# Strided sparse attention and a multiplicative FFN on one core: another order of work at the head

## The chip, the core and the metric

The kernel runs on one core of a Trainium2 chip. TensorE (PE in the profile; PEld is its weight load) multiplies and transposes into PSUM, VectorE (DVE) and ScalarE (ACT) read PSUM and write SBUF, GpSimd (POOL) here casts SBUF to SBUF and sets up masks, SyncE (SP) issues the loads; ACT issues the stores. The metric is device time in microseconds (us) of the one launch, lower is better. One execution is also taken with the profiler; its view gives every instruction a start and a length.

## The reference

Attention over 8 batches of 8 heads, 576 positions of 64 elements; the first four heads see a local band of 32 positions, the other four positions with the same remainder by 32. Its output, laid out as 4608 tokens of 512, goes through a feed-forward part without a nonlinearity but with a product of two projections:

```python
mask_local = (rel >= 0) & (rel < 32)
mask_strided = (rel >= 0) & (pos[None, :] % 32 == pos[:, None] % 32)
scores = np.where(masks[None], q @ k.T / sqrt(64), -1e9)
attn = softmax(scores)
x = (attn @ v).transpose(0, 2, 1, 3).reshape(4608, 512)
a = x @ w1            # 512 x 1024
b = x @ w2            # 512 x 1024
out = (a * b) @ w3 @ w_out    # 1024 x 1024, 1024 x 512
```

All inputs and the output are float32; the kernel computes its products in float16 with sums in float32.

## The kernel before

**Tiles.** Tokens go in nine tiles of 512, batches in eight of 576 tokens, and a batch in four *pairs* of heads: pairs 0 and 1 are local, 2 and 3 strided. w3 and w_out are multiplied once, in the kernel (the *fold*), so that each tile needs three sets of products: a and b (`ab_halves`, sixteen units of four matmuls), and the output products (`o_halves`, eight units of four).

**Loads.** Every load goes through one of nine staging buffers (`stgp`): a DMA issued by SP, then a cast to float16 on POOL or ACT. `load_w3(jc)` takes 128 rows of w3 (4 KB each) into one of four buffers `w3n`; `load_wo(g)` takes 512 KB of w_out in 2 KB rows; `load_w12(g)` takes 256 columns of w1 and of w2, 512 KB each in 1 KB rows, with w1's cast on ACT and w2's on POOL; `load_qk(b, grp)` takes q and k of four heads (512 KB each), `load_rest(b)` the last 64 positions of q and k of all heads, `load_vL` and `load_vS` take V for the local and the strided heads. `load_vL` also has a copy on DVE (line 187) that shifts rows of V after its casts on POOL (line 186).

**Fold.** `fold_tr(jc)` transposes a block of w3 on PE (line 465) and copies it out on DVE and ACT (lines 467, 468); `fold_mm(jc)` gives two half units of four matmuls each (line 443 in the shared helper `acc_halves`) and a copy of the result into `w34`.

**Attention of batches 0 and 1.** `ah_T` transposes q and k of a pair (line 320) and copies them into `qT` and `kT` on ACT; `ah_R` does the same for the rest of a batch. `ah_S` computes the scores in two groups (line 356), the exponential on ACT (line 360) and the mask product on DVE (line 361); `ah_PV` multiplies by V (line 374), and `norm` divides on DVE (lines 384, 385). `ph_T2` transposes the result (line 392) and copies it into `xT`, on ACT for these batches. Scores and products with V share two PSUM buffers (`psB`). The transposes of a pair and the back-transposes share a single one (`psM`), and fold, a, b and output products three (`psF`).

**Order.** PE runs in the order of the program text: each PE instruction is passed to `pe`. The attention of all batches is a list of steps, `stream`; `spread(units, upto, lead)` issues matmul units and, between them, steps of the stream evenly up to position `upto`, where the first `lead` units go without steps. The other engines' instructions are put in order by the framework. Loads go on SP in the order of the text.

In the kernel before, the loads start with w3's block 0 and w_out, then the other blocks of w3 are mixed with batch 0's q, k, v; then come w1 and w2, mixed with batch 1's. The fold is spread over batch 0's attention, then tile 0's a, b products and output products over batch 1's. Tile 1 begins after that, with batch 2's attention between its units, and so on.

In a batch of the stream, pair i's scores come before the back-transposes of pair i - 1, then its products with V, and the transposes of pair i + 2. From batch 2 on another set of functions is used (`ph_...`).

Of the kernel before, what the change touches and what calls it, by code (L numbers as in the profile page):

```python
# [8 lines left out]
FP32 = mybir.dt.float32  # L9
FP16 = mybir.dt.float16  # L10
# [9 lines left out]
def kernel(  # L20
# [11 lines left out]
    nc = tc.nc  # L32
    B, H, S, D = q.shape
# [3 lines left out]
    P = 128  # L37
    NT = 512
    NTILE = NTOK // NT
    KM = DM // P  # L40
    KF = DF // P
# [8 lines left out]
    NM = 512  # L50
# [21 lines left out]
    def copy(eng, out, in_):  # L72
        if eng == "a":
            nc.scalar.copy(out=out, in_=in_)  # L74
        elif eng == "v":
            nc.vector.tensor_copy(out=out, in_=in_)  # L76
        else:
            nc.gpsimd.tensor_copy(out=out, in_=in_)  # L78
# [65 lines left out]
    def load_w3(jc, eng):  # L144
        st = stgp.tile([P, DF], FP32, tag="stg")
        nc.sync.dma_start(st, moe_w3[bass.ds(jc * P, P), :])
        t = ffn.tile([P, DF], FP16, tag="w3n", bufs=4)
        w3n[jc] = t
        copy(eng, t, st)

    def load_w12(g):
        cs = bass.ds(g * 256, 256)
        for wd, wh, eng in ((moe_w1, w1h, "a"), (moe_w2, w2h, "p")):
            st = stgp.tile([P, KM, 256], FP32, tag="stg")
            nc.sync.dma_start(st, wd.rearrange("(c p) n -> p c n", p=P)[:, :, cs])
            copy(eng, wh[:, :, cs], st)


    x16 = {}
# [1 line left out]
    def load_qk(b, grp, engs="pp"):  # L161
        for nm, ten, eng in (("q", q, engs[0]), ("k", k, engs[1])):
            st = stgp.tile([P, 4, 4, D], FP32, tag="stg")
            nc.sync.dma_start(st.rearrange("p h c d -> p h (c d)"),
                              ten[b, 4 * grp:4 * grp + 4, 0:NM].rearrange("h (p c) d -> p h (c d)", c=4))
            t = qkp.tile([P, 4, 4, D], FP16, tag=f"{nm}{grp}")
            copy(eng, t, st.rearrange("p h c d -> p c h d"))
            x16[(b, nm, grp)] = t

    def load_rest(b, eng="p"):  # L170
        st = stgp.tile([P, H, D], FP32, tag="stg")
        for i, ten in enumerate((q, k)):
            nc.sync.dma_start(st[64 * i:64 * i + 64], ten[b, :, NM:S].rearrange("h p d -> p h d"))
        t = qkp.tile([P, H, D], FP16, tag="r")
        copy(eng, t, st)
        x16[(b, "r")] = t

    def load_vL(b):
        vt = v16L[b % 2]
        for hp in range(2):  # L180
            hs = slice(2 * hp, 2 * hp + 2)
            st = stgp.tile([P, 2, LT, D], FP32, tag="stg")
            for h in range(2):
                nc.sync.dma_start(st[32:P, h], v[b, 2 * hp + h].rearrange("(t p) d -> p t d", p=LQ))
            for pr in (bass.ds(32, 32), bass.ds(64, 64)):
                nc.gpsimd.tensor_copy(out=vt[pr, hs, :, 0:D], in_=st[pr])  # L186
            nc.vector.tensor_copy(out=vt[0:32, hs, 1:LT, 0:D], in_=vt[96:P, hs, 0:LT - 1, 0:D])

    def load_vS(b):
        vt = v16S[b % 2]  # L190
        for hp in range(2):
            st = stgp.tile([SQ, 2, ST, D], FP32, tag="stg")
            sf = st.rearrange("p h c d -> p h (c d)")
            sv = v[b, 4 + 2 * hp:6 + 2 * hp].rearrange("h (p c) d -> p h (c d)", c=ST)
            nc.sync.dma_start(sf[0:64], sv[0:64])
            nc.sync.dma_start(sf[64:SQ], sv[64:SQ])
            nc.gpsimd.tensor_copy(out=vt[:, 2 * hp:2 * hp + 2, :, 0:D], in_=st)  # L197
# [114 lines left out]
            norm(s, xps[0:w, :, 0:l * 65], cs[0], l)  # L312

    def ah_T(s):
        ps = psM.tile([P, 2, NM], FP16, tag="m")
        for i, nm in enumerate("qk"):
            src = x16[(s.b, nm, s.hp // 2)]
            h0 = 2 * (s.hp % 2)
            for c in range(4):
                pe(nc.tensor.transpose(ps[:, i, c * P:(c + 1) * P],  # L320
                                       src[:, c, h0:h0 + 2].rearrange("p h d -> p (h d)"), id16))
        for i, t in enumerate((qT, kT)):
            if s.local:
                c0 = 32 * i
                nc.scalar.copy(out=t[:, s.hp, c0:c0 + NM].rearrange("x (p c) -> x p c", c=4),
                               in_=ps[:, i].rearrange("x (c p) -> x p c", c=4))
            else:
                nc.scalar.copy(out=t[:, s.hp, 0:S].rearrange("x (u c w) -> x u c w", u=2, c=4)[:, :, :, 0:64],
                               in_=ps[:, i].rearrange("x (c t u) -> x u c t", c=4, u=2))

    def ah_R(b):
        ps = psM.tile([P, 4, 2, 128], FP16, tag="m")
        pv = ps.rearrange("x g a w -> x (g a w)")[:, 0:512].rearrange("x (g a w) -> x g a w", g=4, a=2)
        src = x16[(b, "r")]
        for g in range(4):
            pe(nc.tensor.transpose(pv[:, g].rearrange("x a w -> x (a w)"),
                                   src[:, 2 * g:2 * g + 2].rearrange("p h d -> p (h d)"), id16))
        for i, t in enumerate((qT, kT)):
            c0 = 32 * i + NM
            nc.scalar.copy(out=t[:, 0:2, c0:c0 + NR], in_=pv[:, 0:2, i])  # L340
            nc.scalar.copy(out=t[:, 2:4, 0:S].rearrange("x g (c w) -> x g c w", w=SQ)[:, :, :, 64:SQ],
                           in_=pv[:, 2:4, i].rearrange("x g (s c) -> x g c s", c=ST))

    def ah_ptm(s, g):
        return ptms[s.hp % 2][:, g * PTG:(g + 1) * PTG]
# [115 lines left out]
    def fold_tr(jc):  # L461
        js = bass.ds(jc * P, P)
        ps = psF.tile([P, 1024], FP16, tag="f", name="trp")
        for kc in range(KF):
            pe(nc.tensor.transpose(ps[:, kc * P:(kc + 1) * P], w3n[jc][:, bass.ds(kc * P, P)], id16))
        pv = ps.rearrange("x (c j) -> x c j", j=P)
        nc.vector.tensor_copy(out=w3T[0][:, :, js], in_=pv[:, 0:4, :])
        nc.scalar.copy(out=w3T[1][:, :, js], in_=pv[:, 4:8, :])
# [13 lines left out]
    def add(f, *a):  # L482
        stream.append(lambda: f(*a))
# [6 lines left out]
    def ph_TS(s, t):  # L490
# [8 lines left out]
        for f in after:  # L499
            f()  # L500

    for p, s in enumerate(pairs):
        b, i = divmod(p, 4)
        if b < AHEAD:
            if i == 0:
                add(ah_T, s)
                add(ah_R, b)
                add(ah_T, pairs[p + 1])
            add(ah_S, s)
            if i:  # L510
                add(ph_T2, pairs[p - 1])
            add(ah_PV, s, 0)
            add(ah_PV, s, 1)
            if i < 2:
                add(ah_T, pairs[p + 2])
            if i == 3:
                add(ph_T2, s)
                batch_end[b] = len(stream)
            continue
        if i == 0 and b == AHEAD:  # L520
            add(ph_TS, None, s)
            gaps(2)
        t = pairs[p + 1] if p + 1 < len(pairs) else None
        add(ph_TS, s, t)
        gaps(1)
        if i or b > AHEAD:
            add(ph_T2, pairs[p - 1])
            if i == 0:
                gaps(1)
                batch_end[b - 1] = len(stream)  # L530
        gaps(1 if i == 0 and b > AHEAD else 2)
        add(ph_PV, s)
        gaps(3)
        if p + 1 == len(pairs):
            add(ph_T2, s)
            batch_end[b] = len(stream)
    pos = [0]

    def spread(units, upto, lead=0):
        n = len(units) - lead  # L540
        p0 = pos[0]
        for i, u in enumerate(units):
            u()
            tgt = p0 + ((upto - p0) * max(i + 1 - lead, 0)) // n
            while pos[0] < tgt:
                stream[pos[0]]()
                pos[0] += 1
# [14 lines left out]
                    x()  # L562


    load_w3(0, "p")
    for g in range(4):
        load_wo(g, "p")
    load_w3(1, "p")
    load_qk(0, 0)
    load_rest(0)  # L570
    load_w3(2, "p")
    load_vL(0)
    load_w3(3, "p")
    load_qk(0, 1)
    load_w3(4, "p")
    load_w3(5, "p")
    load_vS(0)
    load_w3(6, "p")
    load_w3(7, "p")
    load_w12(0)  # L580
    load_w12(1)
    load_w12(2)
    load_qk(1, 0)
    load_rest(1)
    load_w12(3)
    load_vL(1)
    load_qk(1, 1)
    load_vS(1)

    fold = []  # L590
    fold_tr(0)
    for jc in range(KF):
        h0, h1 = fold_mm(jc)
        fold.append(h0)
        if jc + 1 < KF:
            fold.append(lambda jc=jc: fold_tr(jc + 1))
        fold.append(h1)
    spread(fold, batch_end[0], lead=3)
    load_qk(2, 0)
    load_rest(2)  # L600
    load_vL(2)
    units = ab_halves(0) + o_halves(0)
    p0, n = pos[0], batch_end[1] - 1 - pos[0]
    spread(units[0:16], p0 + n * 11 // 19, lead=4)
    load_qk(2, 1)
    load_vS(2)
    spread(units[16:23], p0 + n)
    units[23]()
    stream[pos[0]]()
    pos[0] += 1  # L610
    for tch in range(1, NTILE):
# [47 lines left out]
```

## Time and profile before

| | us |
|---|---|
| median of 3 timed runs | 296.75 (292.37, 296.75, 299.54) |
| the profiled execution | 292.48 |
| span of its instructions | 290.8 |
| start of tile 1's first product | 79.97 |

The busy shares of the span are 91% on PE, 52% each on DVE and ACT, 36% on POOL. The loads move 38.8 MB in, the stores 9.44 MB out. The chain that ended last is 73% PE, 10% ACT, 6% DMA and 6% DVE. The page of the profile shows the span in 40 equal slices of 7.3 us; a digit is the busy share in tenths. The timeline and the groups name an operation by engine, line, output and inputs, shapes (partitions x elements) and count; what stands in brackets is the idle time before and what ended it. A matmul's shown length includes its latency, so the pace of PE is read from the starts of successive ones. "PEclk" or granted clock is the share of TensorE's full clock that the records show.

### The profile page before, as it was taken

The page shows a single profiled execution, that of the slowest core. Times are in us where ns is not written, and L with a number is a line of the kernel's source. Part 1 is how long each engine was busy: PE and PEld are TensorE (multiplying, and loading weights), DVE is VectorE, ACT ScalarE, POOL GpSimd, SP SyncE. Part 2 cuts the span into 40 slices and gives each one's busy share as a digit, 9 for nine tenths or more (in the row PEclk, how much of TensorE's full clock was granted, in tenths as well). Part 3 has the DMA queues.
Part 4 walks back from the last instruction along what each step waited for, and adds up shares of the span by engine and source line. Part 5 has one row for each costly group of instructions (what it writes and reads, how often), then busy time and mean ns, then how long its engine had stood idle before and what let it go on. Part 6 is the DMA issues. An engine that isn't in the chain of part 4 may idle for free.

```text
span 290.8 us, 6556 instructions
## 1 busy us (share of the span) xinstructions
PE 264.0 (91%) x2617; PEld 136.8 (47%) x2617; DVE 150.0 (52%) x293; ACT 151.3 (52%) x305; POOL 103.4 (36%) x118
## 2 busy tenths in 40 slices
PE   2478998879899998999999999999999999999995
PEld 1134564445445554554555455545554554444442
DVE  2014764255747846576476577646645653330320
ACT  2025795827565465656555555565565555323332
POOL 6759544475466536675381535100000000000000
PEclk9997999979999999999999999999999999999999
DMA  7999999999699979996999670120021003003003
GB/s 242 357 224 340 293 348 249 230 267 209 195 291 233 211 172 286 243 243 173 265 265 216 186 216 1 63 87 0 2 80 68 2 0 140 7 0 147 1 0 144
DMA packets 58655, 48.66 MB, mean 167 GB/s; under 512 B 29184, under 2 KB 49664, under 8 KB 58624
## 3 DMA queue, kind: packets, MB, share of 16 engines
q1 hardware_dynamic: 53440, 38.81, 55.0%
q10 hardware_dynamic: 5184, 9.44, 8.9%
q8 instruction: 20, 0.33, 0.5%
q14 instruction: 11, 0.09, 0.1%
HBM read 38.80 MB, written 9.44 MB: 166 GB/s over the span
## 4 chain that ended last, share of the span: by engine, by line
PE 73%; ACT 10%; DMA 6%; DVE 6%; issue 3%; SPq 1%; POOL 0%; ACTq 0%
PE ops L443 22%; PE bps L429 20%; PE aps L420 19%; DMA st<-in_moe_w_dram 3%; PE sps L310 3%; DMA st<-in_moe_w_out_dram 3%; PE ps L392 2%; PE sps L268 2%; ACT xT L399 2%; ACT pte L360 2%; DVE xqs L385 1%; PE pt L225 1%; ACT pte L288 1%; ACT osb L454 1%; PE pt L268 1%
## 5 line engine op out<-in xcount | busy, mean ns | idle before, releaser
L420 PE MATMUL aps<-xT,w1h 128*128 128x512 f16 x288 | 76.2, 382 | 4.3 <-ACT xT L399 4.1
L423 ACT COPY asb<-aps 128x512 f32<-128x512 f32 x72 | 42.5, 590 | 63.8 <-PE aps L420 61.5
L429 PE MATMUL bps<-xT,w2h 128*128 128x512 f16 x288 | 74.3, 380 | 0.0
L431 DVE TENSOR_TENSOR abt<-bps,asb 128x512 f16<-128x512 f32 x72 | 49.5, 688 | 44.9 <-PE bps L429 42.9
L443 PE MATMUL ops<-w,abt 128*128 128x512 f16 x288 | 68.5, 379 | 0.0
L78 POOL CAST t<-st 128x1024 f16<-128x1024 f32 (+1 forms) x48 | 48.5, 1015 | 39.1 <-DMA st<-in_k_dram 21.6
L429 PEld LDWEIGHTS <-w2h 128*128 128x128 f16 x288 | 26.6, 98 | 35.3 <-issue 6.5
L443 PEld LDWEIGHTS <-abt 128*128 128x128 f16 x288 | 25.9, 98 | 27.1
L420 PEld LDWEIGHTS <-w1h 128*128 128x128 f16 x288 | 25.8, 98 | 25.4 <-issue 0.6
L454 ACT COPY osb<-ops 128x512 f32<-128x512 f32 x36 | 21.3, 592 | 29.9 <-PE ops L443 27.3
L186 POOL CAST v16L<-st 32x768 f16<-32x768 f32 (+1 forms) x32 | 27.5, 861 | 16.5 <-DMA st<-in_v_dram 8.5
L288 ACT ACTIVATE pte<-sps 128x960 f16<-128x960 f32 (+1 forms) x24 | 23.8, 990 | 11.8 <-PE sps L268 10.8
L385 DVE TENSOR_TENSOR xqs<-sps,rcp 96x768 f16<-96x768 f32 (+1 forms) x24 | 24.5, 1020 | 0.5
L197 POOL CAST v16S<-st 72x1024 f16<-72x1024 f32 x16 | 16.9, 1059 | 18.2 <-PE pm L310 13.8
L443 PE MATMUL ops<-woh,w3T 128*128 128x512 f16 x64 | 20.2, 446 | 1.7 <-POOL woh L78 1.1
L289 DVE TENSOR_TENSOR ptm<-pte,maskL 128x1152 f16<-128x1152 f16 x12 | 10.0, 832 | 21.8 <-ACT pte L288 21.8
L289 DVE TENSOR_TENSOR ptm<-pte,maskS 72x1152 f16<-72x1152 f16 x12 | 10.2, 854 | 19.5 <-ACT pte L288 19.5
L74 ACT COPY qT<-pt 128x256 f16<-128x256 f16 (+2 forms) x48 | 17.5, 409 | 0.9 <-DVE kT L76 0.9
L310 PEld LDWEIGHTS <-ptm 72*128 72x128 f16 (+1 forms) x336 | 13.6, 97 | 6.3 <-issue 0.6
L392 PEld LDWEIGHTS <-xqs 72*128 72x128 f16 (+1 forms) x224 | 11.9, 98 | 8.8 <-DVE xqs L385 2.3
L392 PE MATMUL ps<-id,xqs 72*128 72x72 f16 (+1 forms) x224 | 13.9, 201 | 1.3 <-DVE xqs L385 1.3
L76 DVE COPY kT<-pt 128x512 f16<-128x512 f16 (+1 forms) x24 | 10.7, 467 | 4.8 <-ACT qT L74 4.8
(76 smaller groups left out, 237.4 us busy)
## 6 DMA issues: line engine op xcount, KB each, us to landing
out_dram<-osb ACTq DMA_DIRECT2D x36, 256.0 KB, 2.0
st<-in_moe_w_dram SPq DMA_DIRECT2D x16, 512.0 KB, 9.1
st<-in_q_dram SPq DMA_DIRECT2D x16, 512.0 KB, 5.6
st<-in_k_dram SPq DMA_DIRECT2D x16, 512.0 KB, 9.3
st<-in_v_dram SPq DMA_DIRECT2D x32, 144.0 KB, 6.8
st<-in_v_dram SPq DMA_DIRECT2D x16, 256.0 KB, 7.3
st<-in_moe_w_out_dram SPq DMA_DIRECT2D x4, 512.0 KB, 7.1
st<-in_q_dram SPq DMA_DIRECT2D x8, 128.0 KB, 7.4
```

Source lines behind the costliest of these rows:

```text
L78: nc.gpsimd.tensor_copy(out=out, in_=in_)
L186: nc.gpsimd.tensor_copy(out=vt[pr, hs, :, 0:D], in_=st[pr])
L288: nc.scalar.activation(out=pte[0:kr, lo:hi], in_=src, func=AF.Exp, bias=0.0, scale=scale)
L310: pe(nc.tensor.matmul(xps[:, h, i * 65:i * 65 + 65], s.ptm[0:kr, c0:c0 + P], vt[0:kr, 2 * (s.hp % 2) + h, c, :], start=True, stop=True))
L385: nc.vector.tensor_mul(s.xqs[0:w, c0:c0 + l].rearrange("p i h d -> p h i d"), xv[:, :, :, 0:D], _ap(rcp, 0, [[rcp.ap[0][0], w], [ST, 2], [ ...
L392: pe(nc.tensor.transpose(ps[:, t * w:(t + 1) * w], s.xqs[0:w, t].rearrange("p h d -> p (h d)"), id16[0:w, 0:w]))
L420: pe(nc.tensor.matmul(aps, w1h[:, ci, bass.ds(jc * P, P)], xT[ci][:, tok], start=(ci == 0), stop=(ci == KM - 1)))
L423: nc.scalar.copy(out=asb, in_=aps)
L429: pe(nc.tensor.matmul(bps, w2h[:, ci, bass.ds(jc * P, P)], xT[ci][:, tok], start=(ci == 0), stop=(ci == KM - 1)))
L431: nc.vector.tensor_mul(abts[tch][:, jc, :], bps, st["asb"])
L443: pe(nc.tensor.matmul(st["ps"], lhs(ci), rhs(ci), start=(ci == 0), stop=(ci == KF - 1)))
L454: nc.scalar.copy(out=osb, in_=ps)
```

## The change

The loads get another order: batch 0's q, k, v first (the first k and the rest of q and k cast on ACT), then all of w1 and w2, then w3's block 0, w_out and the other blocks of w3, then batch 1. `load_w12` takes 512 columns now, in 2 KB rows, as two tiles of 512 KB for each of w1 and w2, and all its casts are on POOL.

Batch 0's attention is issued with nothing between its steps, in two couples of pairs: transposes of both, scores of both, then products with V and back-transposes of each. Its transposes take PSUM from `psF`, and its copies into `kT` go to DVE. Then come all sixteen a, b units of tile 0 in a row. The fold follows: the first 14 of its 24 units in a row, the other ten with 8 of the 20 remaining steps of batch 1. Tile 0's output products lie between the other 12 steps.

```diff
     def load_w12(g):
-        cs = bass.ds(g * 256, 256)
-        for wd, wh, eng in ((moe_w1, w1h, "a"), (moe_w2, w2h, "p")):
-            st = stgp.tile([P, KM, 256], FP32, tag="stg")
-            nc.sync.dma_start(st, wd.rearrange("(c p) n -> p c n", p=P)[:, :, cs])
-            copy(eng, wh[:, :, cs], st)
+        cs = bass.ds(g * 512, 512)
+        for wd, wh in ((moe_w1, w1h), (moe_w2, w2h)):
+            src = wd.rearrange("(c p) n -> p c n", p=P)
+            for c in range(0, KM, 2):
+                st = stgp.tile([P, 2, 512], FP32, tag="stg")
+                nc.sync.dma_start(st, src[:, c:c + 2, cs])
+                copy("p", wh[:, c:c + 2, cs], st)
...
     def ah_T(s):
-        ps = psM.tile([P, 2, NM], FP16, tag="m")
+        pool, tag = (psF, "f") if s.b == 0 else (psM, "m")
+        ps = pool.tile([P, 2, NM], FP16, tag=tag, name="tps")
...
         for i, t in enumerate((qT, kT)):
+            eng = "v" if i and s.b == 0 else "a"
...
+    for i0 in (0, 2):
+        s0, s1 = pairs[i0:i0 + 2]
+        add(ah_T, s0)
+        if i0 == 0:
+            add(ah_R, 0)
+        add(ah_T, s1)
+        for s in (s0, s1):
+            add(ah_S, s)
+        for s in (s0, s1):
+            add(ah_PV, s, 0)
+            add(ah_PV, s, 1)
+            add(ph_T2, s)
+    batch_end[0] = len(stream)
     for p, s in enumerate(pairs):
         b, i = divmod(p, 4)
+        if b == 0:
+            continue
...
+    load_qk(0, 0, "pa")
+    load_rest(0, "a")
+    load_vL(0)
+    load_qk(0, 1)
+    load_vS(0)
+    load_w12(0)
+    load_w12(1)
     load_w3(0, "p")
     for g in range(4):
         load_wo(g, "p")
...
+    for jc in range(1, KF):
+        load_w3(jc, "p")
     load_qk(1, 0)
     load_rest(1)
-    load_w12(3)
     load_vL(1)
     load_qk(1, 1)
     load_vS(1)
...
+    while pos[0] < batch_end[0]:
+        stream[pos[0]]()
+        pos[0] += 1
+    for u in ab_halves(0):
+        u()
+    load_qk(2, 0)
+    load_rest(2)
+    load_vL(2)
+    fold = [lambda: fold_tr(0)]
     for jc in range(KF):
...
-    spread(fold, batch_end[0], lead=3)
...
-    units = ab_halves(0) + o_halves(0)
     p0, n = pos[0], batch_end[1] - 1 - pos[0]
-    spread(units[0:16], p0 + n * 11 // 19, lead=4)
+    spread(fold, p0 + n * 8 // 19, lead=14)
     load_qk(2, 1)
     load_vS(2)
-    spread(units[16:23], p0 + n)
-    units[23]()
+    units = o_halves(0)
+    spread(units[0:7], p0 + n)
+    units[7]()
```

`ah_R` is changed in the same way as `ah_T`.

More of the change, by code (lines that the diff above doesn't have):

```diff
@@ L322, in ah_T @@
         for i, t in enumerate((qT, kT)):
+            eng = "v" if i and s.b == 0 else "a"
             if s.local:
                 c0 = 32 * i
-                nc.scalar.copy(out=t[:, s.hp, c0:c0 + NM].rearrange("x (p c) -> x p c", c=4),
-                               in_=ps[:, i].rearrange("x (c p) -> x p c", c=4))
-            else:
-                nc.scalar.copy(out=t[:, s.hp, 0:S].rearrange("x (u c w) -> x u c w", u=2, c=4)[:, :, :, 0:64],
-                               in_=ps[:, i].rearrange("x (c t u) -> x u c t", c=4, u=2))
+                copy(eng, t[:, s.hp, c0:c0 + NM].rearrange("x (p c) -> x p c", c=4),
+                     ps[:, i].rearrange("x (c p) -> x p c", c=4))
+            else:
+                copy(eng, t[:, s.hp, 0:S].rearrange("x (u c w) -> x u c w", u=2, c=4)[:, :, :, 0:64],
+                     ps[:, i].rearrange("x (c t u) -> x u c t", c=4, u=2))
     def ah_R(b):
-        ps = psM.tile([P, 4, 2, 128], FP16, tag="m")
+        pool, tag = (psF, "f") if b == 0 else (psM, "m")
+        ps = pool.tile([P, 4, 2, 128], FP16, tag=tag, name="rps")
         pv = ps.rearrange("x g a w -> x (g a w)")[:, 0:512].rearrange("x (g a w) -> x g a w", g=4, a=2)
@@ L338, in ah_R @@
         for i, t in enumerate((qT, kT)):
+            eng = "v" if i and b == 0 else "a"
             c0 = 32 * i + NM
-            nc.scalar.copy(out=t[:, 0:2, c0:c0 + NR], in_=pv[:, 0:2, i])
-            nc.scalar.copy(out=t[:, 2:4, 0:S].rearrange("x g (c w) -> x g c w", w=SQ)[:, :, :, 64:SQ],
-                           in_=pv[:, 2:4, i].rearrange("x g (s c) -> x g c s", c=ST))
+            copy(eng, t[:, 0:2, c0:c0 + NR], pv[:, 0:2, i])
+            copy(eng, t[:, 2:4, 0:S].rearrange("x g (c w) -> x g c w", w=SQ)[:, :, :, 64:SQ],
+                 pv[:, 2:4, i].rearrange("x g (s c) -> x g c s", c=ST))
     def ah_ptm(s, g):
@@ L567 @@
         load_wo(g, "p")
[L568 to L582, printed above, removed]
+    for jc in range(1, KF):
+        load_w3(jc, "p")
     load_qk(1, 0)
     load_rest(1)
-    load_w12(3)
     load_vL(1)
@@ L588 @@
     load_vS(1)
-    fold = []
-    fold_tr(0)
+    while pos[0] < batch_end[0]:
[7 more added lines that the diff above has]
+    fold = [lambda: fold_tr(0)]
     for jc in range(KF):
@@ L597 @@
         fold.append(h1)
-    spread(fold, batch_end[0], lead=3)
-    load_qk(2, 0)
-    load_rest(2)
-    load_vL(2)
-    units = ab_halves(0) + o_halves(0)
     p0, n = pos[0], batch_end[1] - 1 - pos[0]
-    spread(units[0:16], p0 + n * 11 // 19, lead=4)
+    spread(fold, p0 + n * 8 // 19, lead=14)
     load_qk(2, 1)
     load_vS(2)
-    spread(units[16:23], p0 + n)
-    units[23]()
+    units = o_halves(0)
+    spread(units[0:7], p0 + n)
+    units[7]()
     stream[pos[0]]()
```

## The prediction

> **What bounds the kernel now.** I read the summary of engines first, then stages of the head (the stretch before tile 1's first product), then the timeline inside it, and last the costliest lines of that stretch.
>
> ```profile
> PE 264.0 (91%) x2617; PEld 136.8 (47%) x2617; DVE 150.0 (52%) x293; ACT 151.3 (52%) x305; POOL 103.4 (36%) x118
> ```
>
> PE is busy 91% of the span, and in the slices of the page 90% or more in nearly all after the first eleven, so a change of order can win or lose only in the head. The busy time of each engine by stage (length, then PE, PEld, DVE, ACT, POOL busy, granted clock, DMA share, GB/s):
>
> ```profile
> 5.50:17.40 11.90, 7.29 (x29) 3.17 (x29) 1.54 (x3) 1.17 (x2) 7.29 (x7) 1.00 1.09 317
> 17.40:25.30 7.90, 5.61 (x37) 3.18 (x35) 1.08 (x3) 3.96 (x10) 5.78 (x7) 0.78 1.18 282
> 25.30:46.00 20.70, 18.51 (x241) 11.44 (x241) 15.25 (x32) 15.33 (x26) 11.65 (x12) 1.00 1.07 326
> 46.00:62.00 16.00, 13.11 (x88) 6.18 (x87) 6.03 (x10) 8.41 (x18) 8.67 (x10) 0.92 1.12 227
> 62.00:80.00 18.00, 17.13 (x192) 9.33 (x191) 11.87 (x26) 11.10 (x20) 10.62 (x11) 0.98 0.97 217
> ```
>
> The reader is to see a DMA share of about 1 in all five: the head is fed by transfers without pause, and PE waits for them up to 25 us and once more around 46 to 62. The timeline shows how those waits look, and where the head ends (start, length, engine, line, operation):
>
> ```profile
> 13.98 3.62 PE L443 MATMUL ops<-woh,w3T 128*128 128x512 f16 x8
> ...
> 17.40 1.06 PE L320 MATMUL ps<-id,t 128*128 128x128 f16 x8
> ...
> 20.53 0.62 PE L465 MATMUL trp<-id,t 128*128 128x128 f16 x8 [2.07 <-POOL t L78]
> ...
> 59.12 0.84 DVE L187 COPY v16L<-v16L 32x640 f16<-32x640 f16 x1
> ...
> 60.20 1.90 PE L420 MATMUL aps<-xT,w1h 128*128 128x512 f16 x4
> ...
> 79.97 1.27 PE L420 MATMUL aps<-xT,w1h 128*128 128x512 f16 x4
> ```
>
> The first line runs eight matmuls in 3.62 us, 0.43 us apart; the chain of waits has groups of four in 0.86 us later, 0.216 us apart. So PE runs at half speed early (the granted-clock column doesn't show it that early). At 60 us it does so again, after PE stood from 58.4 to 60.0 for the copy of V on DVE. Tile 1 starts at 79.97 us; this is the number to compare.
>
> PE work that must be done before tile 1, at full speed: a fold step is eight transposes (0.62) and eight matmuls (1.73), times 8 = 18.8 us. Tile 0's a,b products are 16 x 0.86 = 13.8, its output products 8 x 0.86 = 6.9. Attention of one batch is four transposes of q,k (0.61), the rest (0.39), four score groups (0.43), four products of two halves (0.36 local, 0.41 strided, each half) and four back-transposes (0.42): 9.3. With two batches the sum is 58.1, so the present head loses 79.97 - 58.1 = 21.9 us. By 25.3 us PE has done 20 fold matmuls (4.3), 3 x 0.62, 2 x 0.61 and 0.39, that is 7.8 us of work: 17.5 are lost there. The remaining 4.4 are nearly all the stop at 57 to 62: 2.5 idle and 1.4 at half speed.
>
> **The change, part by part.** *Loads.* The bytes are the same 17.1 MB up to batch 1, and all DMAs stay on SP. w1 and w2 go by 2 KB rows: in the windows of the DMA the 1 KB rows of w1, w2 moved at 348 GB/s (1.5 us each 512 KB), the 2 KB rows of w_out landed 1.34 us apart by the casts that followed them. Eight tiles save 0 to 1.3 us of transfer; I take nothing, since PE work covers it from 28 us on. Four casts of w1 (1.05 us) leave ACT and become POOL casts of 1.04: POOL has one cast of 1.04 for each 1.34 to 1.5 us of landing, so it keeps up.
>
> *When data land.* Batch 0's q,k first group is 1 MB; the first 512 KB of before was cast at 4.38 and the second at 5.62, so with 1 KB rows I take 4.4 and 5.9. The rest (256 KB, 1.4 us at some 190 GB/s) lands at 7.4, V local by 10.4, the second group by 13.5, V strided by 16.5. w1, w2 need 8 x 1.5 us: the first halves by 22.5, all by 28.5. w3 and w_out then take 8 x 1.4 + 4 x 1.4: by 45.5.
>
> *Batch 0's attention, alone on PE.* It has no other work to hide its chain. The durations that matter:
>
> ```profile
> L361 DVE TENSOR_TENSOR ptm<-pte,maskL x8: 444/690/1289, 26.4 to 67.7; 128x576 f16<-128x576 f16 x8
> L385 DVE TENSOR_TENSOR xqs<-xps,rcp x16: 553/620/687, 28.7 to 79.1; 96x384 f16<-96x384 f32 x8, 72x512 f16<-72x512 f32 x8
> L360 ACT ACTIVATE pte<-sps x16: 637/650/720, 25.7 to 75.7; 128x576 f16<-128x576 f32 x8, 72x576 f16<-72x576 f32 x8
> L325 ACT COPY qT<-ps x4: 586/586/618, 18.5 to 55.2; 128x512 f16<-128x512 f16 x4
> ```
>
> First couple of pairs: ACT casts k (1.05) by 7.1, the transposes of pair 0 end at 7.7, the rest at 8.5, pair 1 at 9.5 (1.03 each, as at half speed), copies at 10.1, first exponential at 10.8. From there DVE is the slowest engine: four mask products of 0.69, four reciprocals of 0.18 with four products of 0.55, two V copies of 0.33: 6.3 us, to 17.1. Back-transpose 0.8 at half speed: 17.9. Pairs 2 and 3 stand behind that in PE's order although their data are there: two transposes 2.0, copies and first exponential 1.4, to 21.3; DVE 4 x (0.55 + 0.20 + 0.69) = 5.8, to 27.1; back-transpose 0.8, xT copy on ACT 0.64: products a,b start at 28.5. Lower bound: full speed, mask products at 0.45, no V copy between: 24; but w1, w2's first halves are cast only at 23.8, later if landings mix as badly as they did in before, so 25. Upper bound: mask products at 0.94 (two took 1.87) add 2.0, and the V copies ahead of the kT copies on DVE add 4.9 (below): 35.4. I take 28.5, the value from the median rows. kT copies of batch 0 move from ACT (0.59) to DVE (0.42, the row of the fold's 128x512 copy); beside ACT's own they cost nothing, and serial on ACT they would cost 0.5 for each pair.
>
> *Clock.* The products a,b start on a PE that was half idle. Dense work from 13.15 to 18.46 us was still slow, and after 60.2 it took about 2 us to speed up: a cold stretch of 2.0 to 5.3 us, so 1.0 to 2.7 us lost; I take 1.8. [...]
>
> *Fold and batch 1.* From then on PE has dense work whose data have landed: a,b to 28.5 + 13.8 + 1.8 = 44.1, then five transposes and nine halves of the fold without attention (10.8 us), to 54.9, then fold with batch 1. The casts of w3 blocks 4 to 7 wait on POOL for PE to read blocks 0 to 3 (four buffers): the last can run at 44.1 + 6.8 = 50.9, ends at 52, and q, k and rest of batch 1 queue behind it: cast by 54.7. Their transposes come one fold step later, at 56.4. V local is cast by 58.2 (3.5 on POOL), wanted at 62; V strided by 62.4, wanted at 71. So nothing waits, with 1.7 us to spare at the tightest; the stop at 57 to 62 of before (3.9 us) is gone, as the fold covers it. If that cover fails, it costs up to the 3.9 again. For small stalls I put 1.0 (0.5 left over in before, up to 3).
>
> Sum: 28.5 + (58.1 - 9.3) + 1.8 + 1.0 = 80.1 us, against 79.97. What is gained (3.9) is given up by the lone chain (9.3 us of work in 28.5 us: 19.2 lost against 17.5) and by the second cold start and stalls. From tile 1 on nothing changes. The profiled execution took 292.48 us (span 290.8, 1.7 around it), so 292.6. The three timed runs have their median at 296.75, 4.3 above: 296.9, say 297.
>
> **Rivals.** *Slower: DVE's order.* The V copies of batch 0 come ahead of the kT copies in the text of the program. If they are so on DVE, the kT copy of pair 0 waits until the second V cast (POOL from 8.9, four of 0.87, to 12.4) and two copies of 0.33: 12.7 instead of 7.8, and PE, ACT and exponentials stand behind it: 4.9 us. For it: at 59.12 DVE and then PE did wait for just such a copy. Against it: in before DVE ran the fold's copies ahead of V's. With the mask products at 0.94 it comes to 6.9 + 0.1: 299.5 on the profiled scale, 304 on the median's. It passes 2% when both come together or more than 5.9 us is lost.
>
> *Faster: the lone chain is short.* Attention ends at 25 (the bound set by w1, w2), the cold start costs 1.0, small stalls 0.5: 80.1 - 3.5 - 0.8 - 0.5 = 75.3, so 287.8, or 292 on the median's scale, 1.6% faster. For it: at 20.53 eight transposes took 0.62 in a sparse stretch, where at 17.40 they took 1.06. Against it: DVE's 6 us for each couple.
>
> *POOL holds back batch 1.* If the w3 casts hold q and k more than 1.7 us longer, PE waits for them with only fold work that is behind them in its order: 2 to 3.9 us, 294.6 to 296.5 (299 to 301). That is no change by 2%. That the change does nothing at all would give 297 as well, but PE's order is written out, so I give it no part.
>
> **How the numbers follow.** A measurement of this kernel tells about 2% (5.9 us) from no change. Chances: forecast 0.37, POOL 0.10, short chain 0.20, DVE order and slow chain 0.33. Of the last, 0.03 stays within 2%; slower by mixes of the others adds 0.05 taken from the forecast: slower 0.35. The short chain's 1.6% lies so near 2% that a landing or two decide (and the runs scatter from 292.4 to 299.5): 0.12 of it passes, so faster 0.12. Within 2%: 0.53. Range: from 289 (short chain, 292, less 3) to 307 (304, plus 3); the forecast's own is 293 to 301.
>
> **What would show it.** The first a,b matmul of tile 0 at 28.5 (25 to 35), the first of tile 1 at 80. DVE should be the last releaser of PE up to 28; mask products near 0.69. Matmuls 0.43 apart in the first 2 to 5 us of a,b. No PE wait for w3, w_out or batch 1. An idle DVE before a V copy, with the kT copy behind it, shows the slower rival. I am wrong if tile 1 starts before 74 or after 86, or if anything after it moves.

## The result, and the profile after

The changed kernel took 296.62 us (median of 20 runs, 294.87 to 301.57), the kernel before 294.28 (20 runs, 289.63 to 299.54). The ratio of their undisturbed runs is 1.016 (95% interval 1.0125 to 1.0196), larger than the quotient of the medians because more runs of the kernel before were disturbed. That is slower by less than 2%, so no change by the bound that the prediction set, though with little to spare, and clearly more than nothing. The profiled execution took 295.99 us, its span 294.3, against 290.8 before.

The stages of the changed kernel's head (start and end, length, then PE, PEld, DVE, ACT, POOL busy, granted clock, DMA share, GB/s), cut where its parts begin:

```profile
10.30:20.40 10.10, 3.96 (x56) 2.88 (x56) 8.37 (x16) 3.62 (x6) 9.33 (x10) 1.00 1.07 314
20.40:32.00 11.60, 7.61 (x103) 6.00 (x104) 7.39 (x15) 4.93 (x8) 7.75 (x9) 1.00 1.04 388
32.00:47.70 15.70, 15.70 (x71) 6.89 (x69) 4.84 (x7) 5.33 (x9) 7.03 (x7) 1.00 1.09 364
47.70:60.00 12.30, 11.56 (x93) 6.67 (x91) 4.58 (x10) 4.37 (x8) 10.01 (x11) 1.00 0.96 226
60.00:82.20 22.20, 20.31 (x243) 11.90 (x240) 13.52 (x31) 14.97 (x31) 11.48 (x12) 1.00 0.60 130
```

The first two rows are batch 0's attention, one couple of pairs in each. In the first, DVE is busy 8.4 of 10.1 us and PE 4.0. The third row is tile 0's a,b products without a pause, the fourth the dense part of the fold, the fifth fold and output products with batch 1. From the third on PE is busy 91% or more: the dense work that was to cover the loads does. The timeline of the same execution gives the marks:

```profile
31.97 1.90 PE L426 MATMUL aps<-xT,w1h 128*128 128x512 f16 x4
33.67 1.91 PE L435 MATMUL bps<-xT,w2h 128*128 128x512 f16 x4
35.37 1.08 PE L426 MATMUL aps<-xT,w1h 128*128 128x512 f16 x4
...
47.52 0.61 PE L471 MATMUL trp<-id,t 128*128 128x128 f16 x8
...
59.75 0.61 PE L323 MATMUL tps<-id,t 128*128 128x128 f16 x8
...
82.70 0.81 PE L426 MATMUL aps<-xT,w1h 128*128 128x512 f16 x3
```

Tile 0's a,b start at 31.97, its first two groups of four at half speed (1.70 us from one start to the next, where later groups take 0.86), the fold starts at 47.52, batch 1's first transposes at 59.75, tile 1 at 82.70. Before, tile 1 started at 79.97: in these two executions 2.7 of the 3.5 us lie in the head. Tile 1 itself, from its first a product to tile 2's, took 29.9 us against 29.1: the other 0.8. Every later tile took the same in both.

What held the first couple is in DVE's and POOL's timelines (in brackets, idle time before and what ended it). The first line is ACT's first exponential, the others are the changed kernel's DVE up to the couple's last normalisation:

```profile
10.87 1.20 ACT L366 ACTIVATE pte<-sps 128x576 f16<-128x576 f32 x2
11.00 0.69 DVE L76 COPY kT<-tps 128x512 f16<-128x512 f16 x1 [0.58 <-ACT qT L74]
11.73 0.64 DVE L189 COPY v16L<-v16L 32x640 f16<-32x640 f16 x1
12.40 3.38 DVE L367 TENSOR_TENSOR ptm<-pte,maskL 128x576 f16<-128x576 f16 x3
...
15.91 0.95 DVE L189 COPY v16L<-v16L 32x640 f16<-32x640 f16 x1
16.89 0.46 DVE L367 TENSOR_TENSOR ptm<-pte,maskL 128x576 f16<-128x576 f16 x1
...
19.79 0.98 DVE L391 TENSOR_TENSOR xqs<-xps,rcp 96x384 f16<-96x384 f32 x2
```

and its POOL:

```profile
9.60 3.46 POOL L188 CAST v16L<-st 32x768 f16<-32x768 f32 x4 [3.86 <-DMA st<-in_v_dram]
13.12 2.35 POOL L78 CAST t<-st 128x1024 f16<-128x1024 f32 x2
15.51 1.17 POOL L199 CAST v16S<-st 72x1024 f16<-72x1024 f32 x1
16.94 1.31 POOL L199 CAST v16S<-st 72x1024 f16<-72x1024 f32 x1 [0.26 <-DMA st<-in_v_dram]
```

Three things are to be seen: the kT copy starts only when ACT's qT copy has ended; the two V copies stand among the mask products; and three mask products take 3.38 us, 1.13 each on average, while POOL casts almost without pause, but the fourth, which began at 16.89 in POOL's pause of 0.26, took 0.46, and the cast that began just after it, at 16.94, took 1.31 in place of 1.17.

### The profile page after: what moved, and what is told of

It reads as the page before. It is cut to its first block, busy times and chain, and to the rows that moved or that the text cites. A ratio compares the mean times of both kernels' runs of the same rounds, so it can differ in the third digit from the quotient of the medians.

```text
span 294.3 us, 6561 instructions
## 1 busy us (share of the span) xinstructions
PE 264.3 (90%) x2617; PEld 139.8 (48%) x2617; DVE 157.3 (53%) x299; ACT 147.7 (50%) x297; POOL 105.1 (36%) x120
## 4 chain that ended last, share of the span: by engine, by line
PE 76%; DVE 10%; ACT 8%; issue 2%; DMA 2%; SPq 1%; ACTq 0%; DVEq 0%
PE ops L449 24%; PE bps L435 20%; PE aps L426 19%; PE sps L312 3%; DVE ptm L367 3%; PE ps L398 2%; DVE xqs L391 2%; DMA st<-in_k_dram 2%; ACT qT L74 2%; PE sps L270 2%; ACT osb L460 2%; ACT pte L290 1%; DVE v16L L189 1%; ACT xT L405 1%; PE pt L227 1%
## 5 line engine op out<-in xcount | busy, mean ns | idle before, releaser
L78 POOL CAST t<-st 128x1024 f16<-128x1024 f32 (+1 forms) x46 | 45.9, 1010 | 47.0 <-DMA st<-in_q_dram 16.0
L199 POOL CAST v16S<-st 72x1024 f16<-72x1024 f32 x16 | 17.2, 1082 | 17.0 <-PE pm L312 12.2
L291 DVE TENSOR_TENSOR ptm<-pte,maskL 128x1152 f16<-128x1152 f16 x12 | 11.0, 918 | 21.2 <-ACT pte L290 21.2
L398 PE MATMUL ps<-id,xqs 72*128 72x72 f16 (+1 forms) x224 | 15.4, 208 | 5.2 <-DVE xqs L391 5.2
L291 DVE TENSOR_TENSOR ptm<-pte,maskS 72x1152 f16<-72x1152 f16 x12 | 10.1, 842 | 18.3 <-ACT pte L290 18.3
L398 PEld LDWEIGHTS <-xqs 72*128 72x128 f16 (+1 forms) x224 | 12.3, 101 | 13.1 <-DVE xqs L391 7.1
L449 PE MATMUL ops<-woh,w3T 128*128 128x512 f16 x64 | 15.8, 379 | 0.7 <-DVE w3T L473 0.7
## 6 DMA issues: line engine op xcount, KB each, us to landing
st<-in_moe_w_out_dram SPq DMA_DIRECT2D x4, 512.0 KB, 12.2
```

The lines of the kernel that those rows point to most:

```text
L398: pe(nc.tensor.transpose(ps[:, t * w:(t + 1) * w], s.xqs[0:w, t].rearrange("p h d -> p (h d)"), id16[0:w, 0:w]))
L449: pe(nc.tensor.matmul(st["ps"], lhs(ci), rhs(ci), start=(ci == 0), stop=(ci == KF - 1)))
```

## The experiments

Three theories of why the lone chain came late: **A**, DVE's queue in the first couple; **B**, PE at half speed; **C**, PE's order, with the second couple behind the first. **D** is about tile 1. The line numbers move by a few between the kernels.

Two things limit what the marks below can say. Each mark is from one profiled execution. The changed kernel and two of the runs below (the fold mixed early, batch 2's group earlier) have the same program up to the fold: their first couple ended at 20.77, 20.83 and 20.86, but a,b started at 31.97, 32.89 and 32.07, and the fold at 47.52, 47.96 and 48.31. The start at 32.89 follows a mask product of the second couple that took 1.29 us beside a cast, where the other two have 0.46. So the end of the first couple is good to about 0.1 us, and a start of a,b that differs by less than 0.9 shows nothing by itself. And each ratio is to the kernel before, run beside it; the changed kernel was not run again beside its variants.

**V copies of batch 0 on ACT.**

```diff
-            nc.vector.tensor_copy(out=vt[0:32, hs, 1:LT, 0:D], in_=vt[96:P, hs, 0:LT - 1, 0:D])
+            copy("a" if b == 0 else "v", vt[0:32, hs, 1:LT, 0:D], vt[96:P, hs, 0:LT - 1, 0:D])
```

> The changed kernel with one edit: batch 0's two V copies (0.64 and 0.95 us on DVE between the mask products of pairs 0 and 1) run on ACT. In the changed kernel tile 0's first a matmul starts at 31.97 us and tile 1's at 82.70. Theory A (the lone chain is late because DVE's queue in the first couple holds the V copies and slow mask products): DVE is freed of 1.6 us, a,b start at 30.4, tile 1 at 81.1. Rival B (the clock): DVE's queue is not what ends last, start stays at 31.5 to 32. Rival C (PE's order of the couples): 32.0 too, since the second couple only begins after the back-transposes; if those come earlier by 1.6 the start moves by the same, so C and A both allow 30.4, but under C the idle time of DVE between the couples, some 2.5 us, stays.

The first couple ended at 19.52, 1.25 sooner, tile 0's a,b started at 30.82, 1.15 sooner, and the fold 1.5 sooner (46.02). Ratio to the kernel before 1.0068 (1.0029 to 1.0108), median 295.86. A holds for its part, though not all of the 1.6. In this execution tile 1 started at 82.39, so only 0.3 of it arrived; the mask products of batch 1 took up to 1.14 where they had taken up to 1.00, and PE waited 1.3 us for them after 47 us, not 0.8. The profiled execution (297.40) was the slowest of the ten, though. By the ratio, 1.0068 against 1.0161, more than half of the loss came back, by the medians 0.8 us.

**PE kept busy during batch 0's attention.**

```diff
+    def warm(n):
+        ps = psF.tile([P, 512], FP32, tag="f", name="wps")
+        for _ in range(n):
+            pe(nc.tensor.matmul(ps, id16, wsrc, start=True, stop=True))
...
+            add(ah_S, s)
+            add(warm, 3)
```

> The changed kernel with extra matmuls on PE whose result nobody reads (three of 128x512 after each step of batch 0's attention, six before the first), so that PE is not idle there. Theory B (the clock makes the lone chain late): transposes of pairs take 0.61 in place of 1.06, a,b start by 30.5 or earlier and their first eight matmuls take 1.73 in place of 3.4: tile 1 at 79.5 to 80. Theory A (DVE's queue): the start stays at 31.5 to 32.3, and only the cold start of 1.7 us is saved: tile 1 at 81. If the extra matmuls are themselves in the way, the start is later than 32.3.

The start came at 32.61, 0.6 later, but the cold stretch was gone: the fold started at 46.66, 14.05 us after a,b, in place of 15.55 in the changed kernel. So the cold start cost 1.5 us in this pair. The late start doesn't decide on B, since something else moved in this run: on DVE a V copy now stood ahead of the kT copies.

```profile
11.45 0.33 DVE L197 COPY v16L<-v16L 32x640 f16<-32x640 f16 x1 [8.03 <-POOL v16L L196]
11.70 0.67 DVE L76 COPY kT<-tps 128x512 f16<-128x512 f16 x1
```

The first kT copy came at 11.70 in place of 9.35, and the extra matmuls stood before the first scores, so the first mask product began at 14.94 in place of 12.40. The second couple had no such delay, and its mask products took as long in sum (2.46 against 2.49 us): from its first transposes (22.45) to a,b it took 10.2 us, in place of 10.9. That points to some 0.8 us that half speed on PE costs there; the start of 32.61 is no evidence against B. Ratio 1.0097 (1.0061 to 1.0133), median 297.15; tile 1 at 82.28.

**Pairs in line in place of couples.** The order of batch 0's steps became:

```python
ah_T 0, ah_R, ah_T 1, ah_S 0, ah_S 1, ah_PV 0, ah_T 2, ph_T2 0, ah_T 3, ah_S 2,
ah_PV 1, ph_T2 1, ah_S 3, ah_PV 2, ph_T2 2, ah_PV 3, ph_T2 3
```

> The changed kernel with batch 0's steps in another order: the transposes of pairs 2 and 3 and the scores of pair 2 come before the back-transposes of pair 1, and so on, not in two couples. Theory C (the second couple stands behind the first in PE's order): DVE's idle time between the couples goes, a,b start at 29.5, tile 1 at 80.2. Theory A alone (DVE's queue of the first couple): at most 0.5 is won, start at 31.5. Theory B: PE is busier and may be faster, start near 31.

The start came at 32.29, later than any of the theories said, tile 1 at 83.42, median 296.79, ratio 1.0112 (1.0071 to 1.0153). C falls for this order: DVE's wait moved, as a row of this run's DVE shows:

```profile
25.74 0.89 DVE L367 TENSOR_TENSOR ptm<-pte,maskS 72x576 f16<-72x576 f16 x1 [1.73 <-ACT pte L366]
```

**The fold mixed with batch 1 early.** `lead=14` became `lead=3`.

> The changed kernel with the fold mixed with batch 1 after its first 3 units in place of 14. My step was that the lead of dense fold work covers batch 1's loads (q and k cast at 52 to 54), worth up to 3.9 us. If so, PE now stands before batch 1's first transposes or products with V for 1 to 3.9 us and tile 1 starts at 83.7 to 86.6. Rival: by the time the fold starts (47.5 in the trace) batch 1 has landed anyway, and nothing moves: 82.2 to 83.2.

Tile 1 started at 87.92, 5.2 later, more than expected; from the fold's start on it is 40.0 us in place of 35.2. A wait of PE and the stage of 48 to 60 us in this run:

```profile
PE tps L323 <- POOL t L78: 1.8, 1, 1.8
```

```profile
48.00:60.00 12.00, 9.45 (x68) 5.38 (x67) 2.99 (x6) 3.74 (x9) 6.15 (x7) 0.86 0.92 210
```

PE stood for POOL's cast of batch 1's k, and the clock granted over that stage fell to 0.86: part of the cost is a second cold start. Median 300.04, ratio 1.0174 (1.0104 to 1.0245). That dense work ahead of batch 1 covers its loads in this kernel is shown by the wait. The cover was worth 4.8 us of the head in this execution and 3.4 by the medians; the ratios, 1.0174 and 1.0161, don't tell the two kernels apart.

**kT copies of batch 0 back on ACT.** `"v" if i and s.b == 0 else "a"` became `"a"` in both functions.

> The changed kernel with batch 0's kT copies back on ACT. In the changed kernel each kT copy on DVE started only when ACT's qT copy had ended (8.7 us of DVE waiting in four waits), and took 0.69. Theory A (DVE's queue and this wait lengthen the lone chain): kT ends 0.1 us sooner for each pair and DVE is freed of 3.2 us, but only what lies in DVE's dense part counts: the copy of pair 1 (0.69). a,b start at 31.0 to 31.6 in place of 31.97. My step in the prediction (copies on two engines side by side save 0.5 for each pair): undoing it costs 0.5 for each couple, start at 33.

The start came at 32.68, 0.7 later, tile 1 at 84.84. Whether the copies on DVE are a gain stays open: the first couple ended at 20.21, 0.56 sooner than with them, and behind the later start stands a mask product of the second couple that took 1.14 us, where the changed kernel has 0.46. There is no gain of two engines side by side, since the copies run one after the other:

```profile
DVE kT L76 <- ACT qT L74: 8.7, 4, 5.9
```

This line of the changed kernel's waits (8 to 32 us; total, times, longest) has all four kT copies waiting for qT: the first began at 9.35, when ACT's qT copy from the same PSUM tile (8.74, 0.58 long) had ended at 9.32. The trace shows a wait of one engine for the other, and not its reason. The kernel before shows the same wait in the fold's two copies, from which the prediction took its 0.42:

```profile
14.23 0.42 DVE L467 COPY w3T<-trp 128x512 f16<-128x512 f16 x1 [7.26 <-PE trp L465]
...
14.69 0.59 ACT L468 COPY w3T<-trp 128x512 f16<-128x512 f16 x1 [7.10 <-DVE w3T L467]
```

Median 298.05, ratio 1.0235 with a wide interval (1.0095 to 1.0375).

**POOL relieved.**

```diff
-    load_qk(0, 1)
+    load_qk(0, 1, "aa")
...
-            nc.gpsimd.tensor_copy(out=vt[:, 2 * hp:2 * hp + 2, :, 0:D], in_=st)
+            copy("a" if b == 0 else "p", vt[:, 2 * hp:2 * hp + 2, :, 0:D], st)
```

> The changed kernel with the casts of batch 0's second q,k group and of its strided V (four of 1.0 to 1.2 us on POOL from 13.1 to 18.2) moved to ACT, which is busy 3.6 of 10.5 us there. In the changed kernel a mask product on DVE takes 0.46 us where POOL is idle and 1.13 where POOL casts. Theory A with its cause in POOL beside DVE: the mask products after 13.1 us fall to 0.45 to 0.7, the couple ends 1 us sooner, a,b start at 31. Rival: the mask products are long for another reason (128 partitions) and stay at 1.1; then the start moves later by what the casts hold up the exponentials, 0.5 to 2 us.

This run's DVE:

```profile
12.72 1.33 DVE L367 TENSOR_TENSOR ptm<-pte,maskL 128x576 f16<-128x576 f16 x2
14.47 0.46 DVE L367 TENSOR_TENSOR ptm<-pte,maskL 128x576 f16<-128x576 f16 x1 [0.41 <-ACT pte L366]
```

With POOL idle from 13.4 to 18.7, mask products take 0.46 and the second V copy 0.33, and DVE waits for exponentials: the cause of the long ones is POOL beside DVE, 0.46 us without its casts and 1.13 on average beside them in the changed kernel. How the one holds up the other isn't shown. The first couple ended at 19.55, 1.2 sooner. The start came at 31.22, 0.75 sooner, and yet the fold at 47.89, 0.4 later: the cold stretch was longer, 2.9 us lost in place of 1.75 (start to fold 16.67, less 13.8). Median 296.02, ratio 1.017 (1.0033 to 1.0307).

**Batch 2's second group earlier in the text.** `load_qk(2, 1)` and `load_vS(2)` moved ahead of the fold.

> The changed kernel with batch 2's second q,k group and strided V loaded before the fold in the text of the program in place of after it. In the changed kernel tile 1 took 0.8 us longer than before (from its first a to tile 2's first a), with V copies of 1.2 and 1.05 us on DVE at 98 to 102. Theory D (batch 2's late loads push casts and V copies into tile 1): tile 1's first a stays at 82.7, tile 2's first a comes 0.8 sooner. Rival: nothing moves; the 0.8 comes from the later start itself.

Inconclusive. SP issued that q at 76.87, as late as in the changed kernel (76.49); it waited 12.5 us, by the profile for output stores (`out_dram`), so the text's place didn't decide. Tile 1 started at 83.49 and took 30.5 us. The loads didn't move, so D was not tested. Median 297.86, ratio 1.0228 (1.0094 to 1.0362).

**The kernel before with 2 KB rows alone.**

```diff
-        cs = bass.ds(g * 256, 256)
+        half, h = divmod(g, 2)
+        cs = bass.ds(half * 512, 512)
+        c = 2 * h
...
+            st = stgp.tile([P, 2, 512], FP32, tag="stg")
+            nc.sync.dma_start(st, src[:, c:c + 2, cs])
```

> The kernel before with one part of the change: w1 and w2 loaded in 2 KB rows (512 columns of two row blocks for each tile of 512 KB), casts as before. My step: 2 KB rows save 0 to 1.3 us of transfer for 4 MB. In the kernel before, transfers bound PE at 46 to 62 us, so a saving would show there: tile 1 at 79.97 less 0 to 1.3, ratio 0.995 to 1.000. Rival: rows make no difference at all, ratio 1.000; the a,b products need two tiles each now, and PE doesn't wait for them, as they land by 46.

The DMA's rate in 40 slices of 1.75 us, in this run:

```profile
GB/s 0 279 390 343 394 411 360 304 221 240 160 231 312 345 392 372 198 221 273 385 385 385 385 386 342 323 192 260 290 177 125 161 373 272 186 248 334 173 112 124
```

and in the kernel before:

```profile
GB/s 0 283 359 302 379 419 366 329 181 228 218 207 319 342 393 399 180 212 295 364 353 347 348 348 348 348 213 198 225 311 171 160 277 297 231 217 288 288 169 163
```

The plateau of w1 and w2 rises from 348 to 385 GB/s, 1.1 us for 4 MB, as estimated. No time is seen to come of it: tile 1 started at 81.11, median 293.84 against 293.98, ratio 1.013 with an interval from 0.988 to 1.039, too wide to show a saving of that size.

**V copies and POOL relief together.** The two edits above.

> The changed kernel with both reliefs of DVE at once: V copies of batch 0 on ACT (alone: a,b start 1.15 us sooner) and the casts of the second q,k group and strided V on ACT (alone: 0.75 sooner). Theory A (the 3.5 us by which the lone chain is later than my sum lie in DVE's first couple): the two add to 1.5 to 1.9, a,b start at 30.1 to 30.5. Rival: ACT becomes the engine that ends last with 6 us more on it; start at 31 or later. For the end of the head I expect less than is won in front, since in the runs so far 0.3 of 1.15 arrived at tile 1: tile 1 at 82 to 82.7.

The start came at 30.76, the fold at 47.32, tile 1 at 82.50. PE in this run:

```profile
30.76 1.90 PE L426 MATMUL aps<-xT,w1h 128*128 128x512 f16 x4
32.45 1.91 PE L435 MATMUL bps<-xT,w2h 128*128 128x512 f16 x4
34.16 1.91 PE L426 MATMUL aps<-xT,w1h 128*128 128x512 f16 x4
35.86 1.25 PE L435 MATMUL bps<-xT,w2h 128*128 128x512 f16 x4
```

Three groups and part of the fourth are slow, where the changed kernel had two and little of a third. So the 1.2 won in front was lost again as cold time in this execution, and 0.2 is left at the fold. That is no rule: in the run with the V copies alone on ACT the start was as early (30.82), and full speed came before 34 us. In the first couple the reliefs added in part: its last normalisation on DVE ended at 18.82, where the changed kernel's ended at 20.77, 1.95 us, while alone they won 1.25 and 1.2. In the second couple a mask product of 1.29 gave part of it back. Median 294.67, ratio 1.0085 (1.0039 to 1.0131). The profiled execution (296.33) was the slowest of the five here, too; by the median 1.95 us came back, by the ratio about half of the loss.

**V copies on ACT and PE kept busy.**

> The changed kernel with the V copies of batch 0 on ACT and the extra matmuls that keep PE busy. Alone the first ended tile 0's a,b products 1.5 us sooner, the second 0.9 sooner. If the cold start and DVE's queue are two separate costs, they add: the fold's first matmul at 46.5 in place of 48.87, tile 1 at 80.5 to 81.5. Rival (the last stretch of the head is bound by the chain of batch 1 on DVE and ACT, not by when the fold starts): the fold starts at 46.5 and tile 1 still at 82 to 82.5.

The two gains do not add: the fold started at 46.08, 1.44 sooner (its first product at 47.43, not 46.5), no earlier than with the V copies alone (46.02). The a,b products started at 32.02, 1.2 us later than there, and the cold time that the extra matmuls spared is about as much (1.1). The later start fits a new order on ACT, where the V copy now stood ahead of the remaining qT copies: ACT waited 2.4 us for POOL's cast, ran the V copy at 12.05 and the next qT copy at 12.68, in place of 9.53. Batch 1's transposes came at 58.30. Tile 1 started at 82.36 all the same, as the rival said. Batch 1's mask products and what PE waited for, in this run:

```profile
L375 DVE TENSOR_TENSOR ptm<-pte,maskL x4: 445/460/1799, 64.1 to 71.4; 128x576 f16<-128x576 f16 x4
```

```profile
PE xps L388 <- DVE ptm L375: 1.4, 1, 1.4
```

One mask product took 1.80 us and PE stood 1.4 for it. POOL's casts of batch 1 and 2 run from 56 to 71 us in the changed kernel, too. From the fold's start to tile 1 it was 36.3 us here and 36.4 with the V copies alone, the two runs with the earliest fold, and 35.2 in the changed kernel and with both reliefs. That an earlier chain meets more of the casts fits, but isn't shown. Median 296.76, ratio 1.0138 (1.0093 to 1.0183).

**The kernel before with more cover.** `lead=4` of tile 0's a,b units became `lead=6`.

> The kernel before with the first six a,b units without steps of batch 1 in place of four. In the kernel before PE stood 2.5 us at 57 to 60 for batch 1's V and then ran 1.4 us longer at half speed; my step in the prediction is that dense work ahead of batch 1 covers this. If so, batch 1's steps come 1.7 us later, the stop shrinks to under 1 us, no cold stretch follows: tile 1 at 77 to 78.5, ratio 0.990 to 0.995. Rival: the steps behind get closer together and wait for exponentials and mask products instead: tile 1 at 79.5 to 81.

Tile 1 started at 78.55, 1.4 sooner, but tile 2 at 109.48 against 109.12. The 1.4 is not the edit's: tile 0's a,b, up to which the program is that of the kernel before, already started 2.65 sooner. The first line is this run, the second the kernel before:

```profile
43.38 1.27 PE L420 MATMUL aps<-xT,w1h 128*128 128x512 f16 x4
46.03 1.27 PE L420 MATMUL aps<-xT,w1h 128*128 128x512 f16 x4
```

From there to tile 1 it took 35.2 us in place of 33.9. PE's waits still hold

```profile
PE xps L374 <- DVE v16L L187: 1.8, 1, 1.8
```

where it was 1.6 before, so the stop for V moved with the steps and was not covered. Ratio 1.0009 (0.997 to 1.0049).

**The same with 2 KB rows.**

> The same with w1 and w2 in 2 KB rows. These moved at 385 GB/s in place of 348 in the run with this part alone, 1.1 us for 4 MB, so batch 1's V lands 1.1 us sooner: tile 1 at 76.5 to 78, ratio 0.988 to 0.995. Rival: as in the run with rows alone nothing comes of it, and the two runs of this pair agree within 0.3%.

Tile 1 started at 81.02, 35.2 us after a,b, as with the six units alone. Ratio 1.0022 (0.9984 to 1.006): the rival holds, rows bring nothing that shows. No version run here beats the kernel before.

## Why the prediction was right, and where its sum was not

**No change by 2%: right, with a sum that was 2.6 us short in the head.** It had tile 1 at 80.1 and it came at 82.7. The balance that the forecast rests on, a stop covered and a lone chain that costs as much, held in kind: the stop for V is gone, and the chain cost more than was won.

**The step that was mis-sized** is the first couple: "From there DVE is the slowest engine: four mask products of 0.69, [...] two V copies of 0.33: 6.3 us, to 17.1". DVE was the slowest engine, but from the first exponential at 10.87 to the last normalisation at 20.77 it took 9.9 us. The mask products took 3.84 us in place of 2.76, the V copies 1.59 in place of 0.66; POOL was casting for nearly all of it. The rest, some 1.6, is waits and the kT copy of pair 1, which I had counted at nothing. With it the start was 31.97, not 28.5. The relief of both kinds brought back 1.95 us at the end of this couple, and 1.2 at the start of a,b. So the V copies and POOL's casts are shown as the cause of 1.95 of the 3.6; the rest was not taken apart. By the timed runs the same relief brought the ratio from 1.016 to 1.0085.

**kT copies "cost nothing" beside ACT's**: wrong, they wait for ACT's and took 0.69, not 0.42. The fold's two copies in the kernel before wait for each other in the same way, so its rows could have told. Whether moving them to DVE gained anything is open.

**The second couple**: 10.6 us counted, 10.9 from its first transposes (21.05) to a,b.

**Clock**: 1.8 counted, 1.75 in this execution (47.52 - 31.97 - 13.8). That so close a value came is luck: the same program lost 1.3 and 2.4 in two other executions, and the runs without extra matmuls lost 1.3 to 2.9. The stop before 60.2 us in the kernel before was 0.88 and 1.63 us of idle time, then four matmuls in 1.90; with the early mix one stop of 1.78 us was followed by half speed, eight matmuls in 3.13 where eight take 1.89 later on.

**Fold and cover**: 12.3 counted from the fold to batch 1's transposes, 12.2 measured, and no wait for casts or loads at the transposes. The stop of before at 57 to 62 has no counterpart here; the early mix shows that this kernel needs the cover. In the kernel before, two more units of cover brought nothing.

**Last stretch**: 23.7 counted from those transposes to tile 1, 22.95 measured.

**"From tile 1 on nothing changes"**: off by 0.8. The longer tile 1 stays open: over these kernels it took 28.8 to 31.2 us, and 29.2 in two variants whose tile 1 is the changed kernel's (POOL relieved, kT copies on ACT), so it may be scatter; the run meant to test it didn't move the loads.

**The median of 297** came out near 296.62 by luck, by two errors that cancel: the profiled execution of before stood 4.3 below the median of the first three runs but only 1.8 below that of twenty, and the sum missed 3.5 of span.

**The rivals.** DVE's order: half of it. V copies did come between, but behind the kT copies, so the 4.9 us did not come, while the price of POOL beside DVE came in three of the first couple's four mask products (1.13 us on average, the fourth 0.46); the whole was 3.5. In the run with extra matmuls a V copy did come ahead of the kT copies, and the first of them was 2.35 us later. The short chain had no trace. POOL holding batch 1 did not happen with 14 units of lead, and did with 3.

## What to carry to other kernels

Put a latency-bound chain alone at the head only if its slowest engine is free of everything else: here copies and casts of loads had a large part in DVE's 9.9 us, where 6.3 were counted, and the change gave back what its cover won. Price an elementwise product by rows with and without POOL casting beside it (here 1.13 and 0.46 us), not by the median of both. Don't judge a gain of one us by a mark in one trace: executions of one program here differ by 0.9 us in the start of dense work, by 1.2 in the cold time behind it and, in the kernel before, by 2.65 in the start of a,b. Compare the mark with that of a run with the same program up to there, and check that the profiled execution is not the slowest of its runs.

## What the runs showed of the hardware

- A mask product of 128x576 float16 took 0.44 to 0.46 us beside an idle POOL. Of those that POOL's casts overlapped, in the kernel before and the changed one, two took 0.46 and 0.47 and the others 0.66 to 1.29. V copies of 32x640 took 0.33 beside an idle POOL and, in the changed kernel, up to 1.20 beside a cast.
- PE's cold stretch at the start of a,b cost 1.3, 1.75 and 2.4 us in three executions of the same program, and 1.3 to 2.9 over eight kernels, which alone can hide a gain of one. Extra matmuls in the sparse stretch before kept it away (14.05 us from a,b to the fold, of which 13.8 is work).
- A single stop of 1.78 us of a PE at full speed was followed by half speed (eight matmuls in 3.13 us with the early mix, 1.89 for eight later in that run).
- Two copies, on DVE and on ACT, from one tile in PSUM ran one after the other in both kernels: DVE's from 14.23, 0.42 long, and then ACT's from 14.69 in the kernel before, ACT's from 8.74, 0.58 long, and then DVE's from 9.35 in the changed one.
- Rows of 2 KB against 1 KB: 385 GB/s in the changed kernel and in the kernel before with 2 KB rows alone, against 348 in the kernel before.
- SP's loads of batch 2 stood 12.5 to 12.7 us for output stores, by the profile's inference, in both places that the text gave them.
